# The second matmul of a gated MLP, last two token chunks: as seven block products of Strassen's algorithm

## The chip, the cores and the metric

The kernel runs on one core of one Trainium2 chip. The metric is device time in microseconds (us); the kernel before takes 750.63 us (median of 3 runs, 750.46 to 751.04). The engines that matter are TensorE (PE, matrix products; PEld is its weight load), VectorE (DVE), ScalarE (ACT), GpSimd (POOL) and SyncE (SP), which in this kernel issues the DMA transfers.

## The reference

2048 tokens of width D = 512 go through a layer normalisation, then through two branches whose results are multiplied:

```python
xn = _layernorm(x)
s = attention(xn)          # 32 heads of 16, sliding window of 256, then @ wo
y = _layernorm(xn)
h = gelu(y @ w1 + b1)      # 512 -> F = 1792
g = silu(h @ w2 + b2)      # 1792 -> 512
out = x + s * g
```

All arrays are fp32. The change lies in `h @ w2 + b2` for the last 1024 tokens.

## The kernel before, in words

The tokens are worked in four chunks of 512. The attention comes first, for all tokens (up to about 450 us), and leaves its unnormalised results in memory (`oT_d`, with the softmax denominators in `rden_d`). The MLP and the output projection then go chunk by chunk.

**Precision.** A fp32 product is made as three passes of a reduced format: each operand is split into a high part (a cast) and a low part (operand minus high part), and high×high, high×low and low×high are accumulated in PSUM. So whatever becomes an operand of TensorE must first be split: a cast on ACT or DVE and a subtraction on DVE.

**Chunks 0 and 1.** F is cut into 14 tiles of 128. For each tile f the loop issues the products of w1 (`hidden`, 12 matmuls), gelu on ACT, the split into `gh`, `gl` (`split_g`, line 913), and the products with w2 (`project`, line 919: 4 blocks of 128 tokens × 3 passes = 12 matmuls of 128x512). In the stage of chunk 1, the loop over f (index i) also computes the normalised inputs of chunks 2 and 3 and combinations of them, which the next stage needs.

**Chunks 2 and 3.** The two chunks are 1024 tokens. Their w1 products are already computed together by one level of Strassen's algorithm. The loop runs over g = 0..6; an iteration makes the hidden tiles g and g+7 of both chunks by seven products (`product(j, bank)`, 6 matmuls of 128x512 each, 42 in all). While it does so, DVE and ACT make the combined w1 weights of the next iteration: `combine_w` (line 1029, four 128x256 operations on DVE), `high_w` (line 1039, casts on ACT) and `low_w` (subtractions on DVE). Four results come out: `p1` and `p7` are gelu inputs of chunk 2 (tiles g and g+7), `c12` and `p5` those of chunk 3. Those of chunk 2 are split and multiplied by w2 in the next iteration (24 matmuls, accumulated in `accs`); those of chunk 3 are stored to memory (`g_d`). After the loop comes the output projection of chunk 2, and then a stage for chunk 3 which fetches its gelu results back (`fetch_g`, line 1243), splits them on DVE (`split_last`, line 1237) and multiplies them by w2 (168 matmuls of 128x512).

**The end of a chunk** (`end_chunk`, line 929): DVE adds the bias `b2s` to the four token blocks of `accs`; ACT applies Silu to each and puts the result in the buffer `gated` (128 x 4 x 512); TensorE computes the output projection `s` of four token blocks (12 matmuls each, two PSUM banks `ps_st` in turn); DVE multiplies `s` into `gated`, POOL adds the residual `xo`, and SP stores. Silu and gelu need different function tables in ACT, hence an ACT_TABLE_LOAD at each switch.

**What sets the order.** On PE, DVE, ACT and POOL the instructions run in the order in which the program writes them. A wait of one instruction holds everything behind it on the same engine. The DMA issues on SP are placed by a scheduler, and are also taken in order once placed. `gated` is one buffer for the whole program: outside `end_chunk` its four quarters serve as scratch.

The profile puts nearly all instructions on one line (L43, a helper that records them), so they are told apart by the names of their tiles.

Of the kernel before, what the change touches and what calls it, by code (L numbers as in the profile page):

```python
# [9 lines left out]
F32 = mybir.dt.float32  # L10
# [8 lines left out]
P = 128  # L19
# [31 lines left out]
def mixer_kernel(ctx, tc, x, wqk, wv, wo, w1, b1, w2, b2, out):  # L51
# [850 lines left out]
    def split_o(c, g, raw):  # L902
        ohl = gp.tile([P, 2, 512], F32R, tag="ohl", name=f"ohl_{c}_{g}", bufs=4)
        split(ohl[:, 0], ohl[:, 1], raw, nc.vector.tensor_copy)
        return ohl

    late_w = [*(("w2", f) for f in range(W2_FIRST, NF)), *(("wo", g) for g in range(4))]
# [20 lines left out]

    def end_chunk(c, accs, os_, between):

        us = [accs[i // 2][:, i % 2] for i in range(4)]
        for u in us:
            nc.vector.tensor_add(u, u, b2s)

        def gate(i):
            nc.scalar.activation(gated[:, i], us[i], AF.Silu)

        for i in range(4):
            gate(i)
        for i in range(4):  # L940
            between(i)
            tok = 512 * c + P * i
            xt = load(t2, "t2", x[tok: tok + P, :], f"xo_{c}_{i}")
            ps = ps_st.tile([P, 512], F32, tag="b", name=f"s_{c}_{i}")
            parts = [slice(0, 512)] if c < NCH - 1 or i < 3 else [slice(0, 256), slice(256, 512)]
            for cols in parts:
                k = 0
                for g in range(4):
                    for a, b in PASSES:
                        nc.tensor.matmul(ps[:, cols], os_[g][:, a, P * i: P * (i + 1)], wos[:, b, g, cols],  # L950
                                         start=(k == 0), stop=(k == 11), skip_group_check=True)
                        k += 1
            if c < NCH - 1 or i < 3:
                nc.vector.tensor_mul(gated[:, i], ps, gated[:, i])
                nc.gpsimd.tensor_tensor(xt, xt, gated[:, i], op=ALU.add)
                nc.sync.dma_start(out[tok: tok + P, :], xt)
            else:
                for q in range(2):
                    h = slice(256 * q, 256 * q + 256)
                    nc.vector.tensor_mul(gated[:, i, h], ps[:, h], gated[:, i, h])  # L960
                    nc.vector.tensor_add(xt[:, h], xt[:, h], gated[:, i, h])
                    nc.sync.dma_start(out[tok: tok + P, h], xt[:, h])
# [8 lines left out]
    def inputs(name, kt, part):  # L971

        return area(halves_of[name, kt])[:, 512 * part: 512 * part + 512]
# [52 lines left out]
    def fetch_pair(g):  # L1026
        raw_w[g] = [load(mlp["yp"], "y", w_d["w1"][:, 512 * f: 512 * f + 512], f"wr_{g}_{f}") for f in (g, g + 7)]
# [31 lines left out]
    gated = None  # L1059
    for c in range(2):  # L1060
# [23 lines left out]
        for i in range(NF + 1):  # L1084
# [32 lines left out]
            else:  # L1117
# [37 lines left out]
            steps2(-1)  # L1155

    accs = open_accs(2)
    os_, mine, raws_o = [], {}, []
    NG = NF // 2
    for g in range(NG + 1):  # L1160
        if g < NG:
            if g + 1 < NG:
                fetch_pair(g + 1)
            if g > NG - 3:
                raws_o = [load_o(2, 2 * (g - NG + 2) + k) for k in range(2)]
            banks = [(ps_st if k < 2 else ps_yt).tile([P, 512], F32, tag="b", name=f"p_{g}_{k}") for k in range(4)]
            p1, p5, p7 = (t2.tile([P, 512], F32, tag="t2", name=f"p{k}_{g}") for k in (1, 5, 7))
            u2, c12 = gated[:, 2], gated[:, 3]

            def product(j, bank, more=False):  # L1170

                k = 0
                for kt in range(2):
                    for a, b in PASSES:
                        nc.tensor.matmul(banks[bank], weights(j, a)[:, P * kt: P * (kt + 1)],
                                         inputs(INPUTS[j], kt, b), start=(k == 0 and not more),
                                         stop=(k == 5), skip_group_check=True)
                        k += 1

            def gelu(t, f):  # L1180
                nc.scalar.activation(t, t, AF.Gelu_apprx_tanh, bias=b1s[:, f: f + 1])

            more = g + 1 < NG
            product(0, 0)
            nc.scalar.copy(p1, banks[0])
            product(1, 1)
            nc.vector.tensor_add(p1, banks[1], p1)
            if more:
                combine_w(g + 1)
            for raw, rec in raws_o:  # L1190
                nc.vector.tensor_mul(raw, raw, rec)
            product(2, 2)
            nc.scalar.copy(p5, banks[2])
            gelu(p1, g)
            product(3, 3)
            nc.scalar.copy(p7, banks[3])
            if more:
                high_w(g + 1, 0)
            nc.vector.tensor_add(p5, p5, p7)
            if more:  # L1200
                low_w(g + 1, 0)
            product(4, 0, True)
            nc.scalar.copy(u2, banks[0])
            if more:
                high_w(g + 1, 1)
            nc.vector.tensor_add(p5, p5, u2)
            product(5, 2, True)
            if more:
                high_w(g + 1, 2)
            nc.vector.tensor_add(c12, banks[2], u2)  # L1210
            if more:
                low_w(g + 1, 1)
            gelu(p5, g + 7)
            nc.sync.dma_start(g_d[g + 7], p5)
            product(6, 3, True)
            if more:
                high_w(g + 1, 3)
            nc.vector.tensor_add(p7, banks[3], u2)
            if more:
                low_w(g + 1, 2)  # L1220
                low_w(g + 1, 3)
            gelu(c12, g)
            nc.sync.dma_start(g_d[g], c12)
            gelu(p7, g + 7)
        for k, f in enumerate((g - 1, g + 6)):
            if g:
                project(accs, [(f, mine.pop(f))], 0, NF - 1, range(4) if k == 0 or g == NG else (3, 2, 1, 0))
            if g < NG:
                mine[f + 1] = split_g(2, f + 1, (p1, p7)[k], nc.vector.tensor_copy)
        if g < NG:  # L1230
            for raw, rec in raws_o:
                os_.append(split_o(2, len(os_), raw))

    order = [f for g in range(NG) for f in (g, g + 7)]
    gts = {}

    def split_last(i):

        t = area(i)
        split(t[:, 0:512], t[:, 512:1024], gts.pop(i), nc.vector.tensor_copy)  # L1240
        return t[:, 0:512], t[:, 512:1024]

    def fetch_g(i):
        gts[i] = load(mlp["yp"], "y", g_d[order[i]], f"g_3_{i}")

    for i in range(4):
        fetch_g(i)

    def between(i):
        if i in (1, 2):  # L1250
            mine[i - 1] = split_last(i - 1)
            fetch_g(i + 3)
    end_chunk(2, accs, os_, between)
    accs, os_ = open_accs(3), []
    for i in range(NF):
        if i % 2 == 0:
            project(accs, [(order[k], mine.pop(k)) for k in (i, i + 1)], order[0], order[-1],
                    range(4) if i % 4 == 0 else (3, 2, 1, 0))
        if i + 2 < NF:
            mine[i + 2] = split_last(i + 2)  # L1260
        if i + 6 < NF:
            fetch_g(i + 6)
        if 6 <= i < 10:
            os_.append(split_o(3, i - 6, raw))
        if 5 <= i < 9:
            raw, rec = wanted
            nc.vector.tensor_mul(raw, raw, rec)
        if 4 <= i < 8:
            wanted = load_o(3, i - 4)
    end_chunk(3, accs, os_, lambda i: None)  # L1270


# [31 lines left out]
```

## Time and profile before

| | us |
|---|---|
| median of 3 runs | 750.63 |
| the profiled execution, whole | 750.88 |
| its span in the trace | 749.2 |
| PE busy | 733.9 |
| DVE busy | 511.7 |
| ACT busy | 441.1 |
| POOL busy | 299.3 |

The span is what the trace covers, from the first to the last recorded event; the profiled execution is 1.7 us longer. Busy times are sums over the whole span. In the views quoted below, a row of the chain of waits has a start, a duration, an engine and what it works on; a row of a timeline has a start, a duration, engine, line, operation, output<-input with shape, and in brackets the idle time before it with the engine that ended it; a row of the windows has the stretch, its length, then busy time and count of instructions of PE, PEld, DVE, ACT and POOL, the granted clock, the share of DMA time and GB/s; a row of the groups has busy time, the mean in ns, and the idle time before.

### The profile page before, as it was taken

What the parts mean: (1) busy time and instruction counts of PE and PEld (TensorE: products, weight loads), DVE (VectorE), ACT (ScalarE), POOL (GpSimd) and SP (SyncE); (2) the same over time, 40 slices, a digit from 0 to 9 for tenths busy, and PEclk for the clock granted to TensorE, in tenths of its full rate; (3) what the DMA queues carried; (4) which work ended last, traced back from release to release, by engine and by line L of the source; (5) the groups of instructions that cost most, each with busy time, mean ns of one, the idle gap of its engine ahead of it and who ended that gap; (6) DMA issues with size and microseconds to landing.
All of it is one profiled execution on the core that took longest, in us unless ns stands there. A gap on an engine that the chain in (4) does not pass through costs nothing.

```text
span 749.2 us, 18758 instructions
## 1 busy us (share of the span) xinstructions
PE 733.9 (98%) x7408; PEld 590.4 (79%) x7408; DVE 511.7 (68%) x781; ACT 441.1 (59%) x746; POOL 299.3 (40%) x644
## 2 busy tenths in 40 slices
PE   8999999999999999999999999999999999999997
PEld 7886777777778888777776788888888888888886
DVE  7886777877766778887872648763576765676743
ACT  7757767867667676778877745444463744442001
POOL 7413757767666555767877600120102000001102
PEclk9999999999999999999999999999999999999999
DMA  8633356766555535647724482542012232253611
GB/s 288 191 74 78 84 133 149 201 168 183 152 142 145 144 90 142 162 111 190 200 86 148 133 286 94 165 151 82 31 45 102 93 100 72 70 174 123 222 45 56
DMA packets 56951, 99.40 MB, mean 133 GB/s; under 512 B 11104, under 2 KB 11360, under 8 KB 56864
## 3 DMA queue, kind: packets, MB, share of 16 engines
q1 hardware_dynamic: 56864, 98.21, 45.7%
q8 instruction: 58, 0.95, 0.5%
q14 instruction: 29, 0.24, 0.1%
HBM read 51.39 MB, written 29.62 MB: 108 GB/s over the span
## 4 chain that ended last, share of the span: by engine, by line
PE 89%; ACT 5%; DVE 2%; POOL 2%; issue 1%; DMA 1%; SPq 0%; DVEq 0%; ACTq 0%; POOLq 0%
PE acc L43 20%; PE fb L43 18%; PE zo L43 11%; PE stb L43 9%; PE p L43 9%; PE s L43 6%; PE h L43 6%; PE xy L43 5%; ACT pt L43 4%; PE pv L43 3%; POOL pt L43 1%; DVE xy L43 1%; PE yt L43 1%; DMA x<-in_x_dram 1%; DVE mt L43 0%
## 5 line engine op out<-in xcount | busy, mean ns | idle before, releaser
L43 POOL TENSOR_SCALAR_AFFINE_SELECT pt<-pt 128x256 f32<-128x256 f32 x480 | 193.8, 428 | 132.9 <-ACT pt L43 131.7
L43 ACT ACTIVATE pt<-stb 128x768 f32<-128x768 f32 (+1 forms) x244 | 188.8, 774 | 62.4 <-PE stb L43 54.8
L43 DVE TENSOR_REDUCE mt<-xy 128x4 f32<-128x1024 f32 (+1 forms) x128 | 152.6, 1192 | 4.4
L43 DVE COPY_PREDICATED xy<-upper,zo 128x512 f32<-128x512 int32 x112 | 77.8, 695 | 70.6 <-PE xy L43 63.1
L43 POOL TENSOR_TENSOR xo<-xo,gated 128x512 f32<-128x512 f32 x15 | 20.3, 1358 | 216.8 <-DVE gated L43 192.9
L43 PE MATMUL fb<-xnT,wqb 64*128 64x512 f32 (+1 forms) x684 | 104.8, 397 | 0.3
L43 PE MATMUL zo<-pt,vt 128*17 128x128 f32 x2880 | 103.7, 275 | 0.3 <-POOL pt L43 0.3
L43 PE MATMUL stb<-qk 64*128 64x384 f32 (+1 forms) x488 | 97.2, 393 | 6.2 <-ACT pt L43 4.1
L43 PE MATMUL acc<-w,gh 128*128 128x512 f32 x320 | 98.9, 390 | 0.0
L43 PEld LDWEIGHTS stb<-qk 64*128 64x128 f32 x488 | 45.8, 183 | 51.6 <-ACT pt L43 46.6
L43 PEld LDWEIGHTS zo<-pt,vt 128*17 128x17 f32 x2880 | 67.5, 97 | 15.6 <-issue 6.3
L43 PEld LDWEIGHTS fb<-xnT,wqb 64*128 64x128 f32 (+1 forms) x684 | 64.7, 185 | 11.0 <-DVE pjr L43 1.4
L43 PEld LDWEIGHTS acc<-w,gh 128*128 128x128 f32 x320 | 59.8, 188 | 12.3
L43 PE MATMUL acc<-w,gl 128*128 128x512 f32 x160 | 62.4, 390 | 0.0
L43 PE MATMUL xy<-qk 64*128 64x256 f32 (+2 forms) x536 | 58.4, 291 | 0.2 <-DVE mt L43 0.2
L43 PEld LDWEIGHTS xy<-qk 64*128 64x128 f32 x536 | 46.7, 185 | 6.7 <-issue 3.1
L43 ACT COPY oraw<-zo 128x128 f32<-128x128 f32 x128 | 34.2, 267 | 29.2 <-PE zo L43 28.9
L43 ACT ACTIVATE gated<-acc 128x512 f32<-128x512 f32 x16 | 8.7, 596 | 65.6 <-DVE acc L43 65.6
L43 PE MATMUL s<-wos,ohl 128*128 128x512 f32 (+1 forms) x204 | 44.7, 378 | 0.0
L43 PEld LDWEIGHTS s<-wos,ohl 128*128 128x128 f32 x204 | 36.7, 188 | 7.2 <-DVE gated L43 0.2
L43 PEld LDWEIGHTS zo<-qk 64*128 64x128 f32 x448 | 38.5, 185 | 4.4 <-issue 1.4
L43 ACT COPY p<-p 128x512 f32<-128x512 f32 x21 | 12.3, 586 | 49.7 <-PE p L43 42.3
(195 smaller groups left out, 1241.5 us busy)
## 6 DMA issues: line engine op xcount, KB each, us to landing
qk<-sh SPq DMA_DIRECT2D x128, 128.0 KB
qk<-pjr SPq DMA_DIRECT2D x64, 128.0 KB
oT_d<-oraw SPq DMA_DIRECT2D x32, 256.0 KB
w_d<-in_w_dram SPq DMA_DIRECT2D x14, 512.0 KB
x<-in_x_dram SPq DMA_DIRECT2D x16, 256.0 KB
or<-oT_d SPq DMA_DIRECT2D x16, 256.0 KB
w<-rden_d SPq DMA_DIRECT2D x16, 256.0 KB
xo<-in_x_dram SPq DMA_DIRECT2D x16, 256.0 KB
```

Source lines behind the costliest of these rows:

```text
L43: r = issue(*args, **kwargs)
```

## The change: what it does

The products with w2 of chunks 2 and 3 are computed together by one level of Strassen's algorithm. The matrix of activations (1024 tokens × 1792) is cut into four blocks: chunk (2 or 3) × half of F (tiles g or g+7). The matrix w2 (1792 × 512) is cut likewise: half of F × column half of 256. Seven block products then take the place of eight. Each has 7 steps (g), of 4 token blocks × 3 passes = 12 matmuls of 128x256, 84 per product and 588 in all, in place of 168 + 168 = 336 matmuls of 128x512.

- **Terms of w2.** Four combinations of the quarters of w2 per g. They are made in the loop of chunk 1: at even i `fetch_quarters` loads four 128x256 pieces into `gated[:, 0:2]`, at odd i `combine_terms` makes four subtractions on POOL and stores the result (128x1024, 512 KB) to `t_d` in memory. There is one such buffer, and seven sets go through it.
- **Sums of activations.** In every iteration of the w1 loop POOL makes four 128x512 sums (s1, s2, and in place c12 and p7), and five arrays are stored to `s_d` (the four and p5).
- **Order of the products.** Two of the seven (`plain`) use activations and weights as they are and run in the w1 loop, 24 matmuls per iteration as before but 256 wide. The other five follow the loop, in the code's names: six, five, three, seven with the fourth set of sums, the output projection of chunk 2, seven with the fifth set, the output projection of chunk 3. Their operands are fetched back (35 `fetch_sum`, 14 `fetch_terms`, 256 KB each) and split there: the cast on ACT, the subtraction on DVE.
- **Moved between engines.** In the w1 loop the casts of `split_g` go from DVE to ACT. The loads of attention results for chunk 2 (`load_o`, `split_o`) go from the last two iterations to g = 1..4.
- **Combining the products.** DVE and POOL add the block products with the bias (`lefts`, `rights`, `gated`). The Silu of chunk 2 reads `gated`, that of chunk 3 reads `lefts` and `rights` in halves of 256.

```diff
     def end_chunk(c, accs, os_, between):
-        us = [accs[i // 2][:, i % 2] for i in range(4)]
+        us = [accs[i // 2][:, i % 2] for i in range(4)] if c < 2 else []
...
+    t_d = dram.tile([NF // 2, P, 1024], F32, name="t_d")
+    terms = {}
+
+    def fetch_quarters(g):
+
+        t = terms[g] = gated[:, 0:2].rearrange("p a c -> p (a c)")
+        for k, (f, q) in enumerate(((g, 0), (g + 7, 1), (g, 1), (g + 7, 0))):
+            nc.sync.dma_start(t[:, 256 * k: 256 * (k + 1)], w_d["w2"][:, 512 * f + 256 * q: 512 * f + 256 * (q + 1)])
+
+    def combine_terms(g):
+
+        t1, t2_, t3, t4 = (terms[g][:, 256 * k: 256 * (k + 1)] for k in range(4))
+        for dst, one, two in ((t1, t3, t1), (t3, t2_, t3), (t2_, t2_, t1), (t4, t4, t2_)):
+            nc.gpsimd.tensor_tensor(dst, one, two, op=ALU.subtract)
+        nc.sync.dma_start(t_d[g], terms.pop(g))
...
+                if i < NF:
+                    (combine_terms if i % 2 else fetch_quarters)(i // 2)
...
+    def fetch_terms(g, k):
+        nc.sync.dma_start(area(T_AREAS[g])[:, 512:1024].bitcast(F32), t_d[g][:, 512 * k: 512 * k + 512])
+    def fetch_sum(q):
+        if q < 5 * NG:
+            nc.sync.dma_start(sum_place(q)[1].bitcast(F32), s_d[q // NG, q % NG])
+    def block_product(g, to, left, right, more=False):
+
+        for i in range(4):
+            for k, (a, b) in enumerate(PASSES):
+                nc.tensor.matmul(to(i), left[a][:, P * i: P * (i + 1)], right[b],
...
+        gelu(c12, g)
+        nc.gpsimd.tensor_tensor(s1, c12, p5, op=ALU.add)
+        nc.sync.dma_start(s_d[1, g], s1)
+        gelu(p7, g + 7)
+        nc.gpsimd.tensor_tensor(s2, s1, p1, op=ALU.subtract)
+        nc.sync.dma_start(s_d[0, g], s2)
+        nc.gpsimd.tensor_tensor(c12, p1, c12, op=ALU.subtract)
+        nc.sync.dma_start(s_d[3, g], c12)
+        for k, t in enumerate((p1, p7)):
             if g:
-                project(accs, [(f, mine.pop(f))], 0, NF - 1, range(4) if k == 0 or g == NG else (3, 2, 1, 0))
-            if g < NG:
-                mine[f + 1] = split_g(2, f + 1, (p1, p7)[k], nc.vector.tensor_copy)
+                plain(k, g - 1)
+            mine[g + 7 * k] = split_g(2, g + 7 * k, t, nc.scalar.copy)
+        nc.gpsimd.tensor_tensor(p7, p7, s2, op=ALU.subtract)
+        nc.sync.dma_start(s_d[2, g], p7)
...
+    for g in range(NG):
+        if g == 3:
+            plain(0, NG - 1)
+            plain(1, NG - 1)
...
+        if g + 3 < NG:
+            split_terms(g + 3)
+        split_sum(g + 3)
+        block_product(g, in_two(six), sum_place(g), term(g, 1))
+        fetch_sum(g + 9)
...
+    for g in range(NG):
+        block_product(g, in_pair(five), sum_place(7 + g), term(g, 0))
...
+    for g in range(NG):
+        block_product(g, in_pair(three), sum_place(14 + g), [w2_part(b, 7 + g)[:, 256:512] for b in range(2)])
...
+    for g in range(NG):
+        last_product(3, g)
...
+    end_chunk(2, gated, os_, lambda i: None)
+    os_ = []
+    for g in range(NG):
+        last_product(4, g)
...
+    end_chunk(3, (lefts, rights), os_, lambda i: None)
```

How the instructions stand now, at the places of which the prediction speaks:

POOL, in the stage of chunk 1 (`rsC` is the layer normalisation's root, `xo` the residual of the end of chunk 1). Before:

```order
L43 TENSOR_TENSOR rsC_1_7820<-veC_1_7834,mhalf 128x4
L43 TENSOR_TENSOR rsC_5_8030<-veC_5_8044,mhalf 128x4
L43 TENSOR_TENSOR rsC_6_8087<-veC_6_8101,mhalf 128x4
L43 TENSOR_TENSOR xo_0_8385<-xo_0_8385,gated 128x512
L43 TENSOR_TENSOR xo_1_8407<-xo_1_8407,gated 128x512
```

and of the change:

```order
L43 TENSOR_TENSOR rsC_1_7825<-veC_1_7839,mhalf 128x4
L43 TENSOR_TENSOR gated<-gated 128x256 x8
L43 TENSOR_TENSOR rsC_5_8053<-veC_5_8067,mhalf 128x4
L43 TENSOR_TENSOR gated<-gated 128x256 x4
L43 TENSOR_TENSOR rsC_6_8115<-veC_6_8129,mhalf 128x4
L43 TENSOR_TENSOR gated<-gated 128x256 x16
L43 TENSOR_TENSOR xo_0_8449<-xo_0_8449,gated 128x512
```

Two sets of terms stand ahead of the second `rsC`, one between it and the third, and four behind that, all ahead of the residuals.

ACT, where chunk 1 ends (with what each instruction waits for; `acc` holds the chunk's pre-activations). Before:

```order
L43 CAST gh_13_8342<-g_13_8340 128x512 [waits PE_49,Activation_49]
L43 ACT_TABLE_LOAD
L43 ACTIVATE gated<-acc_0_7724 128x512 [waits DVE_49]
L43 ACTIVATE gated<-acc_0_7724 128x512
L43 ACTIVATE gated<-acc_1_7725 128x512 [waits DVE_49]
```

and of the change:

```order
L43 CAST gh_13_8401<-g_13_8399 128x512 [waits PE_49,Activation_49]
L43 ACT_TABLE_LOAD [waits DMAHW3_49,DMAHW1_49,DMAHW6_49,DMAHW0_49,DMAHW7_49,DVE_49]
L43 ACTIVATE gated<-acc_0_7725 128x512 [waits Pool_49]
L43 ACTIVATE gated<-acc_0_7725 128x512
L43 ACTIVATE gated<-acc_1_7726 128x512 [waits DVE_49]
```

The table load now waits for DMA transfers, which are those that store the terms out of `gated`, and the first Silu for POOL.

DVE, one iteration of the w1 loop, from the sum of `p5` to the next iteration's first (`gh`, `gl`: the splits for w2; `xnT`: low parts of the next w1 weights; `or`, `ohl`: attention results). Before:

```order
L43 TENSOR_TENSOR p_2_8680<-p_2_8680,gated 128x512
L43 TENSOR_TENSOR gated<-p_2_8677,gated 128x512
L43 TENSOR_TENSOR xnT<-ws_0_8696,yh 128x512
L43 TENSOR_TENSOR p_2_8681<-p_3_8678,gated 128x512
L43 TENSOR_TENSOR xnT<-ws_1_8697,wsh 128x512
L43 TENSOR_TENSOR xnT<-wr_10_8673,wsh 128x256
L43 CAST gh_2_8765<-p_2_8679 128x512
L43 TENSOR_TENSOR gl_2_8766<-p_2_8679,gh_2_8765 128x512
L43 CAST gh_9_8781<-p_2_8681 128x512
L43 TENSOR_TENSOR gl_9_8782<-p_2_8681,gh_9_8781 128x512
L43 TENSOR_TENSOR p_3_8793<-p_1_8790,p_3_8793 128x512
```

and of the change:

```order
L43 TENSOR_TENSOR p_2_8769<-p_2_8769,gated 128x512
L43 TENSOR_TENSOR gated<-p_2_8766,gated 128x512
L43 TENSOR_TENSOR xnT<-ws_0_8785,yh 128x512
L43 TENSOR_TENSOR p_2_8770<-p_3_8767,gated 128x512
L43 TENSOR_TENSOR xnT<-ws_1_8786,wsh 128x512
L43 TENSOR_TENSOR xnT<-wr_10_8759,wsh 128x256
L43 TENSOR_TENSOR gl_2_8861<-p_2_8768,gh_2_8860 128x512
L43 TENSOR_TENSOR gl_9_8877<-p_2_8770,gh_9_8876 128x512
L43 TENSOR_TENSOR ohl_1_8882<-or_1_8761,ohl_1_8882 128x512
L43 TENSOR_TENSOR p_3_8896<-p_1_8893,p_3_8896 128x512
```

The two casts have left DVE, and in the iterations g = 1..4 the split of an attention result has come (and a product `or` further ahead). POOL, which had nothing in this loop, now has four operations in each iteration:

```order
L43 TENSOR_TENSOR gated<-gated,p_2_8769 128x512
L43 TENSOR_TENSOR gated<-gated,p_2_8768 128x512
L43 TENSOR_TENSOR gated<-p_2_8768,gated 128x512
L43 TENSOR_TENSOR p_2_8770<-p_2_8770,gated 128x512
L43 TENSOR_TENSOR gated<-gated,p_3_8897 128x512
```

The first row needs the gelu of `c12`, the fourth the splits of `p7` behind it; the fifth is the next iteration's first.

DVE, the last iteration of the w1 loop of the change and what follows it (`xnT` here are the splits of terms and sums for the products after the loop, two DVE subtractions per step of those products; nothing of this stood there before):

```order
L43 TENSOR_TENSOR p_6_9266<-p_1_9263,p_6_9266 128x512
L43 TENSOR_TENSOR xnT<-xnT 128x512
L43 TENSOR_TENSOR p_6_9267<-p_6_9267,p_6_9268 128x512
L43 TENSOR_TENSOR xnT<-xnT 128x512
L43 TENSOR_TENSOR p_6_9267<-p_6_9267,gated 128x512
L43 TENSOR_TENSOR xnT<-xnT 128x512
L43 TENSOR_TENSOR gated<-p_2_9264,gated 128x512
L43 TENSOR_TENSOR xnT<-xnT 128x512
L43 TENSOR_TENSOR p_6_9268<-p_3_9265,gated 128x512
L43 TENSOR_TENSOR gl_6_9364<-p_6_9266,gh_6_9363 128x512
L43 TENSOR_TENSOR gl_13_9380<-p_6_9268,gh_13_9379 128x512
L43 TENSOR_TENSOR xnT<-xnT 128x512 x11
```

Four splits (terms and sums of steps 0 and 1) stand among the additions of the last iteration; those of step 2 and later come behind the splits of `p1` and `p7`.

More of the change, by code (lines that the diff above doesn't have):

```diff
@@ L900, in load_o, with split_o @@
         return raw, rec
-    def split_o(c, g, raw):
+    def split_o(c, g, raw, cast=None):
         ohl = gp.tile([P, 2, 512], F32R, tag="ohl", name=f"ohl_{c}_{g}", bufs=4)
-        split(ohl[:, 0], ohl[:, 1], raw, nc.vector.tensor_copy)
+        split(ohl[:, 0], ohl[:, 1], raw, cast or nc.vector.tensor_copy)
         return ohl
@@ L935, in gate @@
         def gate(i):
-            nc.scalar.activation(gated[:, i], us[i], AF.Silu)
+            if c < 3:
+                nc.scalar.activation(gated[:, i], us[i] if us else gated[:, i], AF.Silu)
+                return
+            for k in range(2):
+                nc.scalar.activation(gated[:, i, 256 * k: 256 * k + 256], accs[k][:, i], AF.Silu)
         for i in range(4):
@@ L1157, in mixer_kernel @@
     accs = open_accs(2)
-    os_, mine, raws_o = [], {}, []
+    os_, mine = [], {}
     NG = NF // 2
-    for g in range(NG + 1):
-        if g < NG:
[L1162 to L1225, printed above, removed]
-            if g:
-                project(accs, [(f, mine.pop(f))], 0, NF - 1, range(4) if k == 0 or g == NG else (3, 2, 1, 0))
-            if g < NG:
-                mine[f + 1] = split_g(2, f + 1, (p1, p7)[k], nc.vector.tensor_copy)
-        if g < NG:
-            for raw, rec in raws_o:
-                os_.append(split_o(2, len(os_), raw))
@@ L1234, in mixer_kernel @@
[L1234 to L1269, printed above, removed]
@@ new lines, in mixer_kernel, with bank2 @@
+    fetch_terms(6, 0)
+    for q in (7, 8, 6):
+        fetch_sum(q)
+    split_terms(2)
+    split_sum(2)
+    bl = b2s[:, 0:256].unsqueeze(1).to_broadcast([P, 2, 256])
+    bd = gated[:, 0, 256:512]
+    lefts = bigp.tile([P, 4, 256], F32, tag="wb0", name="c_left")
+    rights = bigp.tile([P, 4, 256], F32, tag="wb1", name="c_right")
+    halves2 = (slice(0, 2), slice(2, 4))
+    def bank2(x, h):
+        return x[h].rearrange("p (q c) -> p q c", q=2)
+    six = [ps_yt.tile([P, 512], F32, tag="b", name=f"p6_{k}") for k in range(2)]
@@ new lines, in mixer_kernel @@
+    five = ps_mx.tile([P, 2, 512], F32, tag="mx", name="p5")
+    three = ps_mx.tile([P, 2, 512], F32, tag="mx", name="p3")
+    for g in range(NG):
+        block_product(g, in_pair(five), sum_place(7 + g), term(g, 0))
+        fetch_terms(g, 1)
+        fetch_sum(g + 16)
+        split_sum(g + 10)
+        if g < 2:
+            h = halves2[g]
+            nc.vector.tensor_add(lefts[:, h], bank2(six, g), lefts[:, h])
+            nc.gpsimd.tensor_tensor(rights[:, h], lefts[:, h], bd.unsqueeze(1).to_broadcast([P, 2, 256]), op=ALU.add)
@@ new lines, in mixer_kernel @@
+    for g in range(NG):
+        block_product(g, in_pair(three), sum_place(14 + g), [w2_part(b, 7 + g)[:, 256:512] for b in range(2)])
+        fetch_sum(g + 23)
+        split_sum(g + 17)
+        split_terms(g)
+        if g < 2:
+            h = halves2[g]
+            nc.vector.tensor_add(rights[:, h], bank2([five[:, k] for k in range(2)], g), rights[:, h])
+    for k, h in enumerate(halves2):
+        nc.vector.tensor_add(gated[:, h, 256:512], three[:, k].rearrange("p (q c) -> p q c", q=2), rights[:, h])
```

130 lines of the change are left out of this document (129 added, 1 removed).

## The prediction, made before the changed kernel was run

> **What bounds the kernel now.** I read the page first (busy shares, chain by engine), then the chain of waits from the stage of chunk 1 to the end, then the windows of the stages that the change touches.
>
> ```profile
> PE 733.9 (98%) x7408; PEld 590.4 (79%) x7408; DVE 511.7 (68%) x781; ACT 441.1 (59%) x746; POOL 299.3 (40%) x644
> PE 89%; ACT 5%; DVE 2%; POOL 2%; issue 1%; DMA 1%; SPq 0%; DVEq 0%; ACTq 0%; POOLq 0%
> ```
>
> TensorE is busy 98% of the span. The chain from chunk 1's end is TensorE alone:
>
> ```profile
> 560.81 8.16 PE acc L43 x36
> 568.97 10.88 PE s L43 x48
> 579.85 19.04 PE p L43 x84
> 598.89 5.44 PE acc L43 x24
> 604.33 9.52 PE p L43 x42
> ...
> 673.69 10.88 PE acc L43 x48
> 684.57 10.88 PE s L43 x48
> 695.45 38.08 PE acc L43 x168
> 733.53 11.04 PE s L43 x60
> 744.57 0.03 issue
> ```
>
> Each piece starts where the last one ends, so less work on TensorE is time gained, and any wait put into it is time lost. The helpers are not far behind, though. One iteration of the w1 loop, and the stage of chunk 1:
>
> ```profile
> 619.29:634.25 14.96, 14.96 (x67) 12.39 (x67) 9.26 (x18) 6.91 (x12) 0.00 (x0) 1.00 0.24 72
> 514.00:569.00 55.00, 55.00 (x258) 45.75 (x257) 34.35 (x66) 29.81 (x49) 2.05 (x2) 1.00 0.18 58
> ```
>
> Each is PE at 100%, DVE at 62% (9.26 of 14.96, 34.35 of 55.00), POOL all but idle. The change puts work on POOL in both stages.
>
> **Term A, TensorE.** A 512-wide matmul costs 10.88 / 48 = 226.7 ns. The last piece `s` has 36 of them and 24 of 256 columns: (11.04 − 36 × 0.2267) / 24 = 120.0 ns. The change: 588 × 0.1200 = 70.6 us for 336 × 0.2267 = 76.2 us, so **−5.6 us**, not the eighth that the count of products suggests, as half the width costs 53% of the time. The other 128x256 stream gives the upper end:
>
> ```profile
> L43 PE MATMUL pv<-wva,xnT 128*128 128x256 f32 x192 | 25.8, 287 | 0.0
> ```
>
> 25.8 / 192 = 134 ns makes +2.6 us. I take 120, measured on the same kind of stream at the full clock.
>
> The Trainium skill, "TensorE: Matmul & The Clock Gate", section "Back-to-back issue gap", puts the isolated gap at N / 2.4 + 2.5 ns, so 109.2 and 215.8 ns, and the saving at 8.3 us: the sum below would come out 2.7 us lower. Here both widths lie 13.3 ns over N / 2.4 (226.7 − 213.3, 120.0 − 106.7), so the trace decides.
>
> **How POOL and DVE share.** This sets the price of the rest. At the end of chunk 1, where both work:
>
> ```profile
> 572.57 1.67 POOL L43 TENSOR_TENSOR xo<-xo,gated 128x512 f32<-128x512 f32 x1 [36.70 <-DVE gated L43]
> 573.00 1.78 DVE L43 TENSOR_TENSOR xnT<-ws,yh 128x512 fp32r<-128x512 f32 x1
> 483.49 2.55 POOL L43 TENSOR_TENSOR xo<-xo,gated 128x512 f32<-128x512 f32 x2 [21.30 <-DMA w<-rden_d]
> 483.87 1.28 DVE L43 TENSOR_TENSOR xnT<-yt,xnT 128x512 fp32r<-128x512 f32 x2
> ```
>
> and the same operations undisturbed:
>
> ```profile
> L43 POOL TENSOR_TENSOR pjr<-pjr,sh 128x512 fp32r<-128x512 f32 x28 | 35.8, 1279 | 0.3 <-ACT sh L43 0.3
> L43 POOL TENSOR_TENSOR mh<-mt,mh 128x16 fp32r<-128x16 f32 x29 | 6.5, 224 | 2.5
> 622.12 0.69 DVE L43 TENSOR_TENSOR p<-p,p 128x512 f32<-128x512 f32 x1 [1.72 <-PE p L43]
> 622.73 0.42 DVE L43 TENSOR_TENSOR ws<-wr 128x256 f32<-128x256 f32 x1
> 623.06 0.42 DVE L43 TENSOR_TENSOR ws<-wr,wr 128x256 f32<-128x256 f32 x1
> ```
>
> A DVE subtraction with both operands in SBUF takes 0.69 us alone and 1.78 beside a POOL operation; it ends 0.54 us after the POOL one does (574.78 against 574.24), so it ran behind it. With one operand in PSUM (`yt`, two in 1.28 us) it isn't held. POOL's 1.67 is 1.29 and a wait. So **POOL and DVE's SBUF-SBUF operations run one after the other**, and their times add. Start to start such a DVE operation takes 0.61 us (622.12 to 622.73) with 512 columns and 0.33 with 256; a POOL one 1.28 with 512, and by the line through its two widths 0.22 + 240 × 0.00213 = 0.73 with 256.
>
> **Term B, the end of chunk 1.** POOL's third set of terms stands behind this `rsC`:
>
> ```profile
> 529.06 1.05 POOL L43 TENSOR_TENSOR rsC<-veC,mhalf 128x4 f32<-128x4 f32 x1 [26.10 <-DVE veC L43]
> 564.04 1.28 ACT L43 ACT_TABLE_LOAD   x1
> 569.11 1.09 ACT L43 ACTIVATE gated<-acc 128x512 f32<-128x512 f32 x2 [3.79 <-DVE acc L43]
> 571.80 0.69 DVE L43 TENSOR_TENSOR gated<-s,gated 128x512 f32<-128x512 f32 x1 [1.36 <-PE s L43]
> ```
>
> so it starts at 530.1. Five sets then pass through one buffer, each: combine, store, fetch. Combine: 4 × 0.73 = 2.9 alone; each held by the whole of a DVE operation (0.69) 5.7; with DVE 62% busy I take 4.2. For a store and a fetch of 256 KB the queue and the bytes stand here:
>
> ```profile
> 558.27 2.74 SPq L43 DMA_DIRECT2D xo<-in_x_dram  x2
> 560.20:560.60 0.40, 0.40 (x3) 0.36 (x2) 0.40 (x2) 0.09 (x1) 0.00 (x0) 1.00 0.28 103
> 738.50 0.34 SPq L43 DMA_DIRECT2D out_dram<-xo  x1
> 739.50:740.00 0.50, 0.50 (x4) 0.42 (x3) 0.27 (x1) 0.00 (x0) 0.15 (x1) 1.00 1.04 406
> ```
>
> The store is over just past 740.0, some 2.0 us from its issue (bytes still move at 739.50 to 740.00, at 406 GB/s), the fetch by about 560.5, 2.3. At 0.65 us per 256 KB more, a 512 KB store is 2.65; four issues some 0.4 apart and 2 us for the last, a fetch of 3.1. A cycle is 4.2 + 2.65 + 3.1 = 9.95, and the last store lands at 530.1 + 4 × 9.95 + 4.2 + 2.65 = 576.8. Only then come ACT's table load and Silu (now 564.04 and 569.11; ACT's order holds them), 1.28 + 0.55, and DVE's product, 0.69: 579.3. TensorE has two PSUM banks for `s`; its third block (568.97 + 2 × 2.72 = 574.4) waits for that product. **+5 us.** With 2.9 per set all is done by 573 and costs 0; with 5.7 it costs 12. The weights of the w1 loop, cast by ACT behind the Silus, come during the third and fourth block. SP too waits in each cycle, with loads of attention results, `x` and w1 weights behind it; I give the small waits these make **+0.5**.
>
> While TensorE waits 4.9 us, its clock may fall:
>
> ```profile
> 748.00:749.20 1.20, 0.00 (x0) 0.00 (x0) 0.00 (x0) 0.00 (x0) 0.00 (x0) 0.69 0.00 0
> ```
>
> Half a clock from 748.46 on makes this mean, 3.9 us after the last matmul (744.57). If the clock is half for up to as long after work resumes, that costs 0 to 2; I take **+1**.
>
> **Term C, the w1 loop.** TensorE needs 42 × 0.2267 + 24 × 0.120 = 12.40 us per iteration. DVE's, start to start: three additions from PSUM 1.8; `combine_w` 4 × 0.33 = 1.3; nine SBUF-SBUF operations of 512 columns 5.4 (two for p5, three weight lows, two `gl`, `or`, `ohl`); a low part of 256 columns, 0.3: 8.9. POOL: 4 × 1.29 = 5.2. Only the PSUM additions can lie beside POOL, and they come before its first sum is ready, so I add all: 14.04, or **1.64 over TensorE's 12.40 in g = 1..4**. Without `or` and `ohl` (g = 0, 5) 12.84, 0.44 over. The last iteration makes no weights, but its first splits wait for terms that SP fetches behind stores that wait for POOL, and ACT's copy of a product, for which a PSUM bank waits, stands behind these casts: 2.0 by the same row durations. 4 × 1.64 + 2 × 0.44 + 2.0 = **+9.4**. Ends: all PSUM additions beside POOL (14.04 − 1.8 = 12.24) leaves 0; a further wait of half a DVE operation at each POOL one (4 × 0.3 × 6 = 7.2) makes 17. The work is moved, too: ACT gets two casts (6.9 + 1.2 of 12.4) and isn't full.
>
> **Term D, the start of product six.** When the last product of the loop ends, DVE has nine operations to go up to the split that step 2 of six needs (p5, a split, c12, a split, p7, two `gl`, two splits) and POOL four sums between them: 9 × 0.6 + 4 × 1.29 = 10.5. TensorE has two plain products and two steps, 4 × 1.44 = 5.76. **+4.7** (0 if POOL hides, 7 if ACT's casts come in line too). Behind it, a step of 1.44 us wants one to two DVE subtractions (0.6 to 1.2) and as many ACT casts (0.5 each): no wait.
>
> **Sum.** −5.6 + 5 + 0.5 + 1 + 9.4 + 4.7 = +15.0 on 750.9 (the profiled execution, 0.25 over the median): **766**.
>
> **Rivals.**
>
> *Half hidden.* POOL falls half into DVE's idle time, and the terms are in time. For it: DVE idles 38% now. Against: its additions wait for TensorE's products, so the idle time comes in pieces. C: (14.04 − 0.9 − 12.40) × 4 = 3.0, last iteration 1; D 2.3; B 2.5: −5.6 + 0.5 + 3 + 1 + 2.3 + 2.5 = +3.7, **755**.
>
> *Only the products count.* POOL finds its gaps everywhere and the buffer is free in time: −5.6 + 0.5 + 1 = −4.1, **747**. It needs the cycle of terms under 9.0 us (576.8 − 574.4 + 2.5 = 4.9 less over five combines and four transfers) and an iteration of DVE and POOL under 12.40.
>
> *Memory or matmuls after the loop.* Between the loop and the last projection, 49 fetches and 4 outputs of 262 KB go by in some 61 us (420 × 0.12 + 10.9): 228 GB/s. The rate by slices:
>
> ```profile
> GB/s 288 191 74 78 84 133 149 201 168 183 152 142 145 144 90 142 162 111 190 200 86 148 133 286 94 165 151 82 31 45 102 93 100 72 70 174 123 222 45 56
> ```
>
> 18.7 us at 288 GB/s have been had, with other shapes. At 200 GB/s the stretch takes 69 us, +8; so does a matmul at 134 ns (588 × 0.014 = 8.2): **774**. Against both: nine fetches lie ahead, and the 120 ns.
>
> **How the numbers follow.** Forecast 0.66 (its own range 760 to 773, from B's and C's ends taken half each), half hidden 0.13, only the products 0.12, memory or matmuls 0.09. The range 756 to 774 leaves out the faster case and about half of the half-hidden one. This kernel's runs can tell 0.2%, 1.5 us. Faster 0.12; same 0.03 (the edge between the faster and the half-hidden case); slower 0.85.
>
> **What would show it.** A: 256-wide matmuls 120 ns apart. B: a gap before the third `s` of chunk 1, with the table load at about 577 and POOL's last combine ending at about 574. C: DVE operations of 1.7 to 2.0 us in the w1 loop, POOL busy there, iterations of about 14.0 us. D: a wait in six at step 2 for a DVE split. The forecast is wrong if DVE's operations keep 0.69 us beside POOL's, if the last term store lands before 572, or if TensorE waits for fetches in five or three.

## The result and the profile after

The changed kernel takes **768.85 us** (median of 4 runs, 767.01 to 770.29) against 750.55 for the kernel before beside it: 1.024 times as long, 95% interval 1.0219 to 1.0261. The forecast was 766 with a range of 756 to 774. The profiled execution of the change took 770.29 us with a span of 768.6, 19.4 us more than that of before.

The page of the changed kernel, busy times and the chain by engine:

```profile
PE 738.1 (96%) x7660; PEld 603.5 (79%) x7660; DVE 551.1 (72%) x790; ACT 477.1 (62%) x817; POOL 375.4 (49%) x703
PE 69%; DMA 8%; issue 6%; DVE 6%; ACT 5%; POOL 5%; SPq 1%; POOLq 0%; DVEq 0%; ACTq 0%
```

TensorE was 89% of the chain and is 69%; DMA, DVE and POOL stand in it now. TensorE's four largest waits from 480 us on (what it waited for, total, times, longest; the other three make 1.3 us):

```profile
PE acc L43 <- DVE gl L43: 5.6, 1, 5.6
PE s L43 <- DVE gated L43: 3.3, 1, 3.3
PE p L43 <- DVE xnT L43: 3.2, 2, 1.9
PE p L43 <- ACT p L43: 2.6, 3, 1.3
```

The first is in the stage of chunk 1, where the forecast had allowed 0.5 us. The second is the end of chunk 1 (term B), the third product six (D), the fourth the w1 loop (C). The chain, in order of time:

```profile
580.56 2.90 DMA t_d<-gated
583.54 1.28 ACT L43
584.83 0.61 ACT gated L43
585.46 0.70 DVE gated L43
586.21 7.38 PE s L43 x24
...
675.28 4.88 DMA xnT<-t_d
...
682.34 3.71 DMA xnT<-s_d
...
692.69 3.32 PE acc L43 x24
696.01 36.00 PE p L43 x300
```

300 narrow matmuls in 36.00 us are 120.0 ns each: term A as taken. From 696 us to the end there is no wait at all. What came before that, stage by stage, is read best against a kernel without waits (below).

### The profile page after: what moved, and what is told of

The parts are those of the page before. It is cut to its first block, busy times and chain, and to the rows that moved or that the text cites. A ratio compares the mean times of both kernels' runs of the same rounds, so it can differ in the third digit from the quotient of the medians.

```text
span 768.6 us, 19714 instructions
## 1 busy us (share of the span) xinstructions
PE 738.1 (96%) x7660; PEld 603.5 (79%) x7660; DVE 551.1 (72%) x790; ACT 477.1 (62%) x817; POOL 375.4 (49%) x703
## 4 chain that ended last, share of the span: by engine, by line
PE 69%; DMA 8%; issue 6%; DVE 6%; ACT 5%; POOL 5%; SPq 1%; POOLq 0%; DVEq 0%; ACTq 0%
PE fb L43 17%; PE zo L43 11%; PE p L43 11%; PE stb L43 8%; PE acc L43 7%; PE s L43 5%; PE xy L43 5%; ACT pt L43 3%; POOL gated L43 3%; PE pv L43 3%; DMA t_d<-gated 2%; DMA gated<-w_d 2%; POOL pt L43 1%; SPq L43 1%; PE h L43 1%
## 5 line engine op out<-in xcount | busy, mean ns | idle before, releaser
L43 PE MATMUL acc<-w,gh 128*128 128x512 f32 (+1 forms) x320 | 86.7, 359 | 0.0
L43 PE MATMUL p<-xnT 128*128 128x256 f32 (+1 forms) x434 | 81.3, 311 | 4.5 <-DVE xnT L43 3.2
L43 PEld LDWEIGHTS p<-xnT 128*128 128x128 f32 x434 | 60.2, 194 | 9.5 <-DVE xnT L43 3.6
L43 PEld LDWEIGHTS acc<-w,gh 128*128 128x128 f32 x320 | 57.9, 194 | 8.6
L43 PE MATMUL acc<-w,gl 128*128 128x512 f32 (+1 forms) x160 | 57.7, 361 | 5.6 <-DVE gl L43 5.6
L43 PE MATMUL s<-wos,ohl 128*128 128x512 f32 (+1 forms) x204 | 46.7, 388 | 3.3 <-DVE gated L43 3.3
L43 ACT CAST xnT<-xnT 128x512 fp32r<-128x512 f32 x62 | 36.3, 616 | 21.4 <-DMA xnT<-s_d 8.4
```

Of the source, the lines that this page charges most:

```text
L43: r = issue(*args, **kwargs)
```

## The experiments

Differences are of medians. The kernel before was timed beside each of the three sets of runs (750.58 to 750.95); the changed kernel was timed only beside 750.55, so a difference to it can be off by the 0.4 us between the sets.

**The terms left out.** The quarters of w2 are neither loaded nor combined nor stored; the products fetch as many bytes of w2 itself.

```diff
-                if i < NF:
-                    (combine_terms if i % 2 else fetch_quarters)(i // 2)
-        nc.sync.dma_start(area(T_AREAS[g])[:, 512:1024].bitcast(F32), t_d[g][:, 512 * k: 512 * k + 512])
+        nc.sync.dma_start(area(T_AREAS[g])[:, 512:1024].bitcast(F32), w_d["w2"][:, 512 * (g + 7 * k): 512 * (g + 7 * k) + 512])
```

> Left out: the terms of w2 are not made (no quarters fetched, no subtraction on POOL, no store in the stage of chunk 1); the products after the loop fetch as many bytes of w2 itself in their place. Theory: the stage of chunk 1 is late by 8.4 us (input rows of chunk 3 behind the term transfers on SP, then TensorE idle 5.7 us and a half clock) and its end by 5.2 us (Silu behind the last store of terms); both go, so 768.9 - 13.6 = about 755 us. Rival 1: only the end of the stage is the terms' doing and the late input rows are not: about 763.6. Rival 2: the waits come back in the w1 loop, which POOL and DVE bound: 762 or more.

Measured 755.97 us (755.38 to 756.66; 1.0072 of before, 1.0057 to 1.0087): 12.9 less than the change. The waits for `gl` and for `gated` are gone, those of the loop and of six stay: the theory, and neither rival.

**The sums left out.** The four POOL operations of each iteration go; the stores take `p1`, `p5`, `p7`, `c12` as they are.

```diff
-        nc.gpsimd.tensor_tensor(s1, c12, p5, op=ALU.add)
-        nc.sync.dma_start(s_d[1, g], s1)
+        nc.sync.dma_start(s_d[1, g], c12)
...
-        nc.gpsimd.tensor_tensor(p7, p7, s2, op=ALU.subtract)
```

> Left out: the four sums of activations on POOL; the arrays are stored to memory unsummed, as many bytes. Theory (POOL and DVE's SBUF-SBUF operations take turns): the waits in the w1 loop (3.7 us) go, and of the 7.2 us at the start of product six some 5, since DVE's nine operations there are 5.4 us against 5.8 of TensorE: about 760 us. Rival (the waits are for stores and fetches on SP's queue, or for ACT's casts, and POOL's operations lie beside DVE's): 766 to 769.

Measured 758.04 us (756.86 to 758.62; 1.0097, 1.0082 to 1.0112): 10.8 less. All that TensorE still waits for from 480 us on:

```profile
PE acc L43 <- DVE gl L43: 5.0, 1, 5.0
PE s L43 <- DVE gated L43: 3.2, 1, 3.2
```

The loop and six run without a wait once POOL's sums are gone, though the fetches and ACT's casts are the same. That ends the rival by which six waits for these alone.

**Neither.** Both edits together.

> Left out: both the terms of w2 and the sums on POOL, as in the two kernels before. Theory: only the saving of the narrower products and some 1 to 2 us of waits stay: 750.6 - 5.6 + 1.5 = about 746.5 us, faster than the kernel before. Rival (the stretch of five products after the loop costs something of its own, by fetches or by matmuls above 120 ns): 750 or more.

Measured 745.05 us (745.01 to 745.09; 0.9926, 0.9909 to 0.9942), 5.5 less than before. Of the forecast's terms only A shows in this kernel's time, and its chain of waits is TensorE alone:

```profile
568.59 10.88 PE s L43 x48
579.47 19.04 PE p L43 x84
...
667.80 2.88 PE acc L43 x24
670.68 36.05 PE p L43 x300
...
738.78 0.03 issue
```

The last matmul ends at 738.78 against 744.57 before: 5.8 us, of which 0.4 is an earlier start of this stretch. So the stretch of five products costs nothing of its own, and the third rival of the prediction falls. The two halves add: 12.9 + 10.8 = 23.7, and 768.85 − 745.05 = 23.8.

**POOL busy for nobody.** Unsummed arrays are stored, and POOL makes as many 128x512 operations per iteration into scratch that nothing else reads.

```diff
-        nc.sync.dma_start(s_d[1, g], s1)
+        nc.sync.dma_start(s_d[1, g], c12)
...
-        nc.sync.dma_start(s_d[0, g], s2)
-        nc.gpsimd.tensor_tensor(c12, p1, c12, op=ALU.subtract)
+        nc.sync.dma_start(s_d[0, g], p1)
+        nc.gpsimd.tensor_tensor(s1, s1, s2, op=ALU.subtract)
+        nc.gpsimd.tensor_tensor(s2, s1, s2, op=ALU.subtract)
...
-        nc.gpsimd.tensor_tensor(p7, p7, s2, op=ALU.subtract)
```

> Left out: what the sums are for. POOL makes as many 128x512 operations in each iteration, into scratch that nothing else reads, and unsummed arrays are stored. Theory (turn-taking of POOL and DVE): nearly the waits of the changed kernel, 766 to 769 us. Rival (the waits come from stores queued behind POOL's sums, so from the data): like the kernel without sums, about 760.

Measured 766.70 us (765.64 to 767.56; 1.0214, 1.0199 to 1.0229). Of the 10.8 us that the sums cost, 8.7 stay when no data depend on them. So most of it is the turn-taking of POOL with DVE, and only some 2 us are the data (stores behind POOL's sums). Not all of the 8.7 is shown to be turn-taking: POOL still reads `c12`, `p5` and `p1` here, and ACT waits once, 1.5 us, until it has.

**Two blocks of the output projection ahead of six.** They need only attention results, and the two PSUM banks of `s` are free there.

```diff
+    for i in range(2):
+        made_s[2, i] = s_block(2, i, os_)
     six = [ps_yt.tile([P, 512], F32, tag="b", name=f"p6_{k}") for k in range(2)]
```

> The changed kernel, with the first two blocks of the output projection of chunk 2 (24 matmuls of 128x512, 5.44 us, which need only attention results) issued right behind the w1 loop, ahead of product six; nothing is left out. Theory (at the start of six TensorE has 5.8 us of work while POOL and DVE need some 10.5): 5.4 of the 7.2 us go, about 763.5 us. Rival (what six waits for is fetched or cast late and only moves behind): 767 or more.

Measured 762.88 us (761.12 to 764.23; 1.0157, 1.0139 to 1.0176): 6.0 less, the theory. In its trace six runs without a wait. A small new wait shows where the blocks were taken from: between the last product and the third block now lie additions on DVE with nothing to cover them (1.4 us on TensorE). The end of chunk 1, which the edit does not touch, also waits less in this trace (1.5 us for 3.3), so single traces of these kernels differ by a few us there.

**The sums on DVE.** The same operations in the same places.

```diff
-        nc.gpsimd.tensor_tensor(s1, c12, p5, op=ALU.add)
+        nc.vector.tensor_tensor(s1, c12, p5, op=ALU.add)
```

(and so the other three)

> The changed kernel, with the four sums of each iteration on DVE in place of POOL, at the same places; nothing is left out. Theory (turn-taking: a sum holds DVE for 1.29 us on POOL, and for 0.6 us on DVE itself): DVE 8.9 + 2.4 = 11.3 us per iteration, below TensorE's 12.4, so the loop's 3.7 us go; at six nine operations and four sums make 7.8 us against 5.8, so 5 of the 7.2 go: about 760 us. Rival (DVE at 72% is full as it is, and more work on it only delays): 769 or more.

Measured 759.84 us (758.14 to 763.41; 1.0111, 1.0094 to 1.0127): 9.0 less, by giving the busier engine more to do. No wait in the loop is left, and 0.9 us in six and just behind it. The rival, a full DVE, falls.

**The terms on DVE, at the same places.**

```diff
-            nc.gpsimd.tensor_tensor(dst, one, two, op=ALU.subtract)
+            nc.vector.tensor_tensor(dst, one, two, op=ALU.subtract)
```

> The changed kernel, with the four subtractions of each set of terms on DVE in place of POOL, at the same places; the sums stay on POOL; nothing is left out. Theory (the one buffer turns round in combine + store + fetch, the combine stands on POOL behind the normalisation's root, and the rows of chunk 3 wait on SP behind these transfers): combine 1.3 in place of 4 us and not behind the root, so the rows come in time and the last store ahead of the chunk's last products: the 13.6 us go, about 756 us, like the kernel without terms. Rival (transfers on SP alone hold the rows up, whoever combines): 763 or more.

Measured 762.05 us (760.25 to 762.70; 1.0144, 1.013 to 1.0158): 6.8 less, half of the 13 us, so between the theory and its rival. In its trace SP issues chunk 3's rows at the time of before (rows of SP's queue, then DVE):

```profile
520.93 1.82 SPq L43 DMA_DIRECT2D y<-in_x_dram  x4
522.85 3.06 SPq L43 DMA_DIRECT2D gated<-w_d  x4
...
530.87 1.80 DVE L43 TENSOR_TENSOR gated<-gated 128x256 f32<-128x256 f32 x4 [0.30 <-DMA gated<-w_d]
```

but DVE, in its written order, now waits 0.3 us for the quarters that were fetched behind them and works 1.8 us on their combine, with a `gl` behind it; TensorE still waits 2.3 us for that `gl` and 2.0 at the end of the chunk. So the transfers alone do not hold the rows up, as the rival had it; what is left in the middle of the stage is DVE's order.

**All three.**

> The three edits before together: terms and sums on DVE, two blocks of the output projection ahead of product six; nothing is left out. Theory: near the kernel with neither terms nor sums, 745 to 747 us, faster than the kernel before (750.6). Rival (DVE becomes the bound, with some 44 of 55 us in chunk 1 and 11.3 of 12.4 in an iteration): 750 or more.

Measured 753.65 us (752.89 to 754.06; 1.0034, 1.0022 to 1.0047): not the 745 to 747 of the theory. The loop and six have no wait; chunk 1 has those of the kernel just before (1.6 us for `gl`, 2.2 at its end), and the third block of `s` that of the early blocks (1.4).

**All three, with the terms spread.** One early block in place of two, other steps for the sets, two of the seven sets in small tiles in place of Silu's buffer, and each set stored in two halves.

```diff
-                if i < NF:
-                    (combine_terms if i % 2 else fetch_quarters)(i // 2)
+                if i in (1, 3, 6, 7, 9, 11, 13):
+                    combine_terms((1, 3, 6, 7, 9, 11, 13).index(i))
+                if i in (0, 1, 5, 6, 7, 9, 11):
+                    fetch_quarters((0, 1, 5, 6, 7, 9, 11).index(i))
...
-        t = terms[g] = gated[:, 0:2].rearrange("p a c -> p (a c)")
+        t = terms[g] = ([t2.tile([P, 512], F32, tag="t2", name=f"tm_{g}_{k}") for k in range(2)] if g in (4, 6)
+                        else [gated[:, k] for k in range(2)])
```

> Terms and sums on DVE, one block of the output projection of chunk 2 (2.7 us) ahead of product six, and the sets of terms spread otherwise: fetched at steps i = 0, 1, 5, 6, 7, 9, 11 and combined at 1, 3, 6, 7, 9, 11, 13, so that none is fetched beside chunk 3's rows, and the fifth and seventh set in two small tiles in place of the buffer that Silu writes; nothing is left out. Theory (the terms cost by where they stand: beside the rows, and under Silu's buffer): no wait above 1 us is left, 745 to 748 us, faster than the kernel before (750.6 to 751). Rival (DVE or the transfers are the bound in chunk 1, wherever the sets stand): 750 or more.

Measured **747.13 us** (746.23 to 747.73; 0.995, 0.9936 to 0.9964): faster than both kernels, as the theory said. TensorE's waits from 480 us on, and one iteration of the loop:

```profile
PE h L43 <- ACT g L43: 0.5, 2, 0.4
615.86:628.28 12.42, 12.42 (x68) 10.76 (x67) 12.28 (x24) 8.98 (x17) 0.00 (x0) 1.00 0.59 203
```

DVE is busy 12.28 of 12.42 us and holds nothing up. That leaves 2.1 us to the kernel with neither terms nor sums, which also leaves out their work.

**The terms alone spread.** The same schedule and tiles with terms on DVE, the rest as in the change.

> The changed kernel with the terms alone changed: on DVE and spread as in the run before, sums on POOL, nothing moved ahead of six; nothing is left out. Theory: like the kernel without terms (756.0), 755 to 757.5 us, against 762.05 with the terms on DVE at the old places. Rival: what the terms read and write costs by itself, 760 or more.

Measured 757.72 us (757.0 to 758.99; 1.0094, 1.008 to 1.0108), 0.2 above the range of the theory and 1.75 above the kernel without terms. So 11.1 of the 12.9 us were the engine and the place of the terms, not what they read and write. One thing of the expectation did not come about: SP's scheduler put the set meant to come after chunk 3's rows right behind them, in this trace too:

```profile
521.09 1.82 SPq L43 DMA_DIRECT2D y<-in_x_dram  x4
523.00 3.06 SPq L43 DMA_DIRECT2D gated<-w_d  x4
```

What helped in the middle of the stage was therefore the combine's later place in DVE's order (behind the `gl`, which TensorE now awaits 0.4 us in place of 2.3). At the end of the stage it was the earlier sets or the other buffer; the two were not tried apart.

**Another place for the attention results** (from the kernel without terms; the low parts are left out in effect, as the expectation says).

```diff
-        raw = load(t2, "t2", oT_d[g, :, 0:DH, cols], f"or_{c}_{g}")
+        ohl = gp.tile([P, 2, 512], F32R, tag="ohl", name=f"ohl_{c}_{g}", bufs=4)
+        raw = ohl[:, 1].bitcast(F32)
+        nc.sync.dma_start(raw, oT_d[g, :, 0:DH, cols])
```

> The kernel without terms (756.0), and the attention results of chunk 2 loaded into the tile that takes their split in place of the ring of five tiles that p1, p5 and p7 use (the product with the denominators is rounded, so their low parts are left out in effect). Theory (in g = 1..4 these loads take a fourth tile per iteration, so that ACT's copies of the first products wait for the store of POOL's last sum): the waits of TensorE for ACT's copies in the loop, some 2.6 us, go: about 753.4 us. Rival (POOL's last sum is late for the ring of three tiles too): 755.5 or more.

Measured 755.45 us (753.84 to 756.87; 1.0061, 1.0045 to 1.0077) against 755.97: the ranges of the runs overlap, and by time it is the rival. The trace tells more. ACT's waits for the store of a sum (9.8 us in the kernel without terms) are gone, but TensorE's waits are now spread evenly over the iterations, in this window of one:

```profile
611.40:624.20 12.80, 12.69 (x67) 10.69 (x66) 12.40 (x18) 8.22 (x16) 7.16 (x4) 1.00 0.48 164
```

12.80 us, 0.4 over TensorE's own 12.42 in the kernel with the terms spread and the sums on DVE. So in the steady iteration POOL and DVE together need 12.8 us, and the ring of tiles only gathered the excess in a few waits.

## Why the prediction was right, point by point

The chain of the kernel with neither terms nor sums has no waits in it, so its pieces are the measure for the waits of the change, stage by stage (A against before, the others against that kernel):

| | predicted | measured | from |
|---|---|---|---|
| A, narrower matmuls | −5.6 | −5.8 | last matmul 738.78 for 744.57 |
| middle of chunk 1 | +0.5 | +8.8 | `s` begins at 577.36 for 568.59 |
| B, end of chunk 1, with the clock | +6 | +5.3 | `s` takes 16.23 us (577.36 to 593.59) for 10.88 |
| C + D, loop and six | +14.1 | +11.2 | 593.59 to 696.01 is 102.4 us for 91.2 (579.47 to 670.68) |
| sum | +15.0 | +19.5 | the profiled execution: +19.4 |

**A was right**, with the 120 ns of the nearest row (300 matmuls in 36.00 us), not the 134 ns of `pv`. The estimate of 109.2 ns by the gap formula of the Trainium skill ("TensorE: Matmul & The Clock Gate", "Back-to-back issue gap") stays 10.8 ns under the trace in the changed kernel too.

**The step that failed is "SP too waits in each cycle … I give the small waits these make +0.5".** The mechanism was named, its size was not worked out. In the trace of the change, SP's queue, then DVE and POOL:

```profile
510.04 1.75 SPq L43 DMA_DIRECT2D gated<-w_d  x4
520.37 0.32 SPq L43 DMA_DIRECT2D t_d<-gated  x1
522.96 1.74 SPq L43 DMA_DIRECT2D gated<-w_d  x4
...
525.51 2.63 SPq L43 DMA_DIRECT2D y<-in_x_dram  x4
...
531.87 0.69 DVE L43 BATCH_NORM_STATS2 bnC<-y 128x6 f32<-128x512 f32 x1 [6.15 <-DMA y<-in_x_dram]
...
537.27 0.68 DVE L43 TENSOR_TENSOR gl<-g,gh 128x512 fp32r<-128x512 f32 x1
...
516.24 4.10 POOL L43 TENSOR_TENSOR gated<-gated 128x256 f32<-128x256 f32 x4 [9.11 <-DMA gated<-w_d]
535.53 1.11 POOL L43 TENSOR_TENSOR rsC<-veC,mhalf 128x4 f32<-128x4 f32 x1 [15.18 <-DVE veC L43]
```

and the same rows before:

```profile
520.60 1.76 SPq L43 DMA_DIRECT2D y<-in_x_dram  x4
...
525.42 0.69 DVE L43 BATCH_NORM_STATS2 bnC<-y 128x6 f32<-128x512 f32 x1
...
530.22 0.69 DVE L43 TENSOR_TENSOR gl<-g,gh 128x512 fp32r<-128x512 f32 x1
```

The second set's store waits for POOL until 520.37. The third set's fetch may only follow when that store has landed (522.96), and chunk 3's input rows stand behind that fetch on SP: issued 4.9 us late, used by DVE 6.45 us late. DVE keeps its order, so the `gl` for TensorE behind the statistics is 7.05 late, and TensorE waits 5.6 us and then runs at a lower clock. The prediction had counted SP's queue as a cost of the terms and not asked what each load behind it is needed for. The second set is late itself because its fetch, issued at 510.04, lets POOL start only 6.2 us later; the sets fetched from 542.81 on took 3.4 to 3.6 us. Why this one was slower was not tried.

**B was right in mechanism and near in size.** POOL's combines took 3.2 to 4.5 us (4.2 taken) and the cycle (577.33 − 546.26) / 3 = 10.4 (9.95). The last store is 6.7 us later than forecast, since the cycle hung on `rsC` (535.53 for 529.06), and TensorE is 8.8 us later, since it hung on the `gl`; both were late for the same input rows. So TensorE waits 3.3 us and not 5, and the clock after it costs 1.5 us and not 1 (last section). That one delay offsets most of the other is luck: the forecast had neither.

```profile
546.26 3.50 POOL L43 TENSOR_TENSOR gated<-gated 128x256 f32<-128x256 f32 x4 [3.38 <-DMA gated<-w_d]
577.33 3.20 POOL L43 TENSOR_TENSOR gated<-gated 128x256 f32<-128x256 f32 x4 [6.45 <-DMA gated<-w_d]
```

**C was too large, D too small by the clock, the turn-taking right.** From the changed kernel's timelines of POOL and DVE in a steady iteration and at the start of the next (each is stretched by the other), and its windows of that iteration and of the time around six:

```profile
642.90 3.83 POOL L43 TENSOR_TENSOR gated<-gated,p 128x512 f32<-128x512 f32 x2 [5.89 <-ACT gated L43]
644.25 3.03 DVE L43 TENSOR_TENSOR gl<-p,gh 128x512 fp32r<-128x512 f32 x2 [0.37 <-ACT gh L43]
647.20 1.78 DVE L43 TENSOR_TENSOR ohl<-or,ohl 128x512 fp32r<-128x512 f32 x1
...
657.06 3.04 DVE L43 TENSOR_TENSOR gl<-p,gh 128x512 fp32r<-128x512 f32 x2 [0.37 <-ACT gh L43]
...
640.99:653.40 12.41, 12.41 (x68) 10.75 (x68) 12.00 (x18) 8.34 (x15) 7.16 (x4) 1.00 0.54 187
...
678.70:696.01 17.31, 12.82 (x86) 11.85 (x86) 13.13 (x17) 9.74 (x18) 6.99 (x5) 0.90 0.80 295
```

The step "I add all: 14.04" was wrong: POOL's four sums do not all fall on DVE's time. DVE's time that they hold is what its stretched operations show, here about (3.03 − 1.29) + (1.78 − 0.69) + 0.5 of a `ws` (0.91 for 0.42) = 3.3 us, not 5.2, since POOL's sums run in part while DVE waits or adds from PSUM, and are stretched themselves (7.2 us by the window, not 5.2). DVE also waits 0.37 for ACT's cast. With DVE's 8.9 that makes 12.6; from one `gl` to the next it is 657.06 − 644.25 = 12.8, as in the window of the last experiment. So an iteration needs 0.4 us more than TensorE's 12.4, not 1.64. TensorE itself took 12.41 for this one, but the `gl` starts 3.26 us after the iteration here (640.99) and 3.66 after the next (653.40): DVE falls 0.4 us further behind each time, until TensorE has to wait.

Of the 11.2 us, by the starts of the matmuls, 3.8 lie in the loop (9.4 predicted, 2.0 of them in the last iteration, which took 0.3) and 7.4 at six. At six the gaps between the matmuls make 4.5 us, near the 4.7 of the forecast; the other 2.9 are half a clock behind them (1.7, last section), for which the forecast had given nothing here, and restarts of the stream, not taken apart. The path is also longer than forecast: ACT's casts wait for terms and sums whose fetches stand on SP behind stores that wait for POOL (675.28 and 682.34 in the chain), and DVE waits for these casts. The forecast had named that for the last iteration, and for six only as an end of its range.

So the total was near partly by errors of opposite sign: 8.3 us too little in the middle of chunk 1, 0.7 too much at its end and 2.9 too much after it. The rivals: the faster one needed a cycle of terms under 9.0 us and an iteration under 12.40, and they are 10.4 and 12.8. The half-hidden one falls as a whole (755 us; the sums alone cost 10.8, where it gave them 6.3), but in the loop its 4.0 us were nearer than the forecast's 9.4: there POOL did fall partly into DVE's idle time. The third is ruled out by the waitless stretch after 696 us.

## What to carry to other kernels

An operation moved to an idle POOL is not free when DVE works in SBUF beside it: POOL's 1.3 us held DVE, and 0.6 us on DVE itself was cheaper, though DVE was the busier engine by the page. A buffer that passes through memory (combine, store, fetch) in an in-order queue delays every load behind it: list those loads, and who needs each, before giving them a small number. And ask which other user of the buffer inherits its last store; here it was Silu.

## What the runs showed that was not expected

After waits TensorE ran at half its rate, and not only after long ones. The granted clock is the last but two figure of a row (the last row is in product six):

```profile
538.80:544.20 5.40, 5.40 (x15) 4.20 (x15) 3.53 (x11) 3.79 (x7) 2.30 (x3) 0.58 0.30 110
582.90:586.20 3.30, 0.06 (x1) 0.00 (x0) 0.69 (x1) 2.65 (x4) 0.00 (x0) 1.00 0.86 317
586.20:588.10 1.90, 1.89 (x7) 1.52 (x8) 0.67 (x2) 1.90 (x5) 1.29 (x1) 0.91 0.00 0
588.10:591.60 3.50, 3.50 (x11) 2.73 (x9) 3.50 (x6) 0.65 (x2) 1.50 (x1) 0.56 0.65 225
690.19:693.60 3.41, 3.41 (x16) 3.41 (x17) 3.41 (x6) 0.62 (x1) 0.53 (x1) 0.50 0.85 281
```

After the 5.6 us wait in chunk 1 the matmuls run at 0.58 until 544. After the wait of 3.3 us at the end of chunk 1 they start near full rate (0.91 over 1.9 us), and then fall to 0.56 for 3.5 us, with TensorE busy. At six no single wait reaches 2 us, but TensorE did only two matmuls in the 4.4 us before 690.19, and then ran at 0.50 for 3.4 us. The price is (1 − 0.58) × 5.4 = 2.3 us, (1 − 0.56) × 3.5 = 1.5 us and (1 − 0.50) × 3.4 = 1.7 us on top of the waits: about 5.5 of the 19 us. Why the second drop comes late, and what sets off the third, was not tried. The Trainium skill ("TensorE: Matmul & The Clock Gate", "Part 1: The HAM clock gate (the "warmup" mystery)") speaks of an idle window of about 3.4 us; the second drop here followed a wait of 3.3 us, and the third had no wait of 2 us before it.
